# Thresholded attention with a gated mix: the phases of a product apart, and column tiles for attention's remainder

## The chip, the core and the metric

The kernel runs on one core of a Trainium2 chip, with TensorE (PE in the profile), VectorE (DVE), ScalarE (ACT), GpSimd (POOL) and SyncE (SP), which issues the DMAs. What counts is the device time of one execution in microseconds; the median of several runs is given.

## What is computed

Eight batches, eight heads of 576 positions with 64 values each. Attention keeps only the scores within `tau` of a row's largest; its output is the input of a gated mix with two 512x512 products.

```python
scores = scale * np.matmul(q, k.transpose(0, 1, 3, 2))
thresh = np.max(scores, axis=-1, keepdims=True) - tau
scores = np.where(scores >= thresh, scores, -1000000000.0)
attn = np.exp(scores - np.max(scores, axis=-1, keepdims=True))
attn = attn / (np.sum(attn, axis=-1, keepdims=True) + 1e-09)
x = np.matmul(attn, v)              # heads side by side: (B, S, 512)
for k in range(K):                  # K = 5, causal
    gate_pre += conv_w[k][None, None, :] * xp[:, k:k + S, :]
gate = 1.0 / (1.0 + np.exp(-gate_pre))
return gate * (x @ w_val) @ w_out
```

## The kernel before

A **job** is one pair of heads of one batch, 32 in all. Its rows of scores are worked on in tiles of 128 rows (288 tiles): PE makes a tile's scores out of `k` and `q` (line 572, two matmuls of 288 columns that run side by side, one on the upper 64 rows of the array and one on the lower, in two banks of one PSUM room), DVE scales them and finds the largest (579), ACT takes the exponential (593), DVE masks and sums (601), PE turns the result (686, transposes of 64 columns), ACT copies it to `T` (698, 702, 706), and PE multiplies `T` with `v`. That last product, **attention**, has four blocks of 128 keys for each of two heads, each with 64 columns of the array (lines 734 and 768), and a remainder of 64 keys a head, which stand together in one block of 128 and are multiplied by one matmul over all 128 columns (727 and 760). The first jobs do this half by half (`attended`), the jobs from tile 41 on with both halves at once (`attended_at_once`), in one PSUM room. DVE divides the result (740, 776), and ACT, DVE and POOL make its convolution (`convolve`), its gate, and two parts, `xh` and `xl`, whose sum is the value.

After the four jobs of a batch come eight **products** (`products`, line 923): four with `w_val` (`wv` in the program's names), then four with `w_out` (`wo`), each of 128 output features and both halves of the positions. A product is 48 matmuls of 64x128 weights and 288 columns, in pairs: one on the upper 64 rows of the array, one on the lower. As both write all 128 partitions, the two of a pair go to different banks, and every bank needs both. So there are two phases, `turn` 0 and 1: in the first the upper rows write bank 0 and the lower bank 1, in the second the other way round. Between the phases stands a drain of PE. Each phase is two operations of 6 pairs (`AT_ONCE = 2`), and each operation follows the one before (`last`), over products and batches, too. DVE then multiplies the product with the gate (959), or ACT or DVE scale it for the output (1023, 1025).

The order on every engine is set by a planner that runs while the program is built (`carry_out`). Each operation has an engine, a cost, operations that it follows, rooms that it takes and gives, and a due time: the number of its tile plus an offset from a table, `EARLY` for tiles under 69 and `AT` for the others. The planner lets its own clock run, and gives the engine that is free first the operation with the least due time of those that could begin. What it emits is fixed; on the chip every engine goes through its list in order and waits for semaphores. Four PSUM rooms of two banks, `u`, serve scores, transposes, attention and products alike. Several operations may go to one of two or three engines, as the small add that makes the threshold, `th`.

```python
cost = 0.39 * AT_ONCE + (DRAIN if turn and not c0 else 0.0)
last = [op("PE", k, cost, done, run, after, [] if turn or c0 else [r_acc])]
k += PACE_M
```

## Time and profile before

| | |
|---|---|
| median of 3 runs | 723.87 us (721.24 to 723.91) |
| the profiled execution | 722.67 us |
| its span, first to last instruction | 720.8 us |
| PE matmul busy | 683.0 us, 95% of the span |
| PE weight loads busy (PEld) | 524.4 us, 73% |
| DVE busy | 642.5 us, 89% |
| ACT busy | 514.3 us, 71% |
| POOL busy | 258.6 us, 36% |

Shares are of the whole span and mix stages with different limits: a start of about 140 us in which weights are prepared and the first jobs run, a long even stage, and an end of some 37 us with products alone. Matmuls are pipelined and their ends are modelled, so two that follow each other overlap in the records; what a piece costs PE is read from starts. The granted clock is 0.983 of full speed in the mean, 1.00 from 200 us on.

### The profile page before, as it was taken

How to read it: one execution, taken by the hardware profiler on the slowest of the kernel's cores; microseconds unless marked ns; L12 is line 12 of the kernel's file. 1: busy time of each engine (PE TensorE's matmuls, PEld its weight loads, DVE VectorE, ACT ScalarE, POOL GpSimd, SP SyncE). 2: the span in 40 equal slices, each digit the busy share in tenths (PEclk: the TensorE clock that was granted, in tenths of full speed). 3: DMA queues.
4: the chain of work that ended last, by engine and by line, in shares of the span. 5: the costliest groups of instructions: out<-in, count | busy, mean ns of one | idle time of the engine just before them, and what ended most of it. 6: DMA issues, size and time to landing. Idle time of an engine off the chain costs nothing.

```text
span 720.8 us, 21163 instructions
## 1 busy us (share of the span) xinstructions
PE 683.0 (95%) x8470; PEld 524.4 (73%) x8470; DVE 642.5 (89%) x1709; ACT 514.3 (71%) x937; POOL 258.6 (36%) x420
## 2 busy tenths in 40 slices
PE   8787789889999999999999999999999999999997
PEld 5444456667677787777777787777877877777887
DVE  6999789998899998899899998999999998999642
ACT  6887687777877787677776787777776877777520
POOL 2453444564223423324222432235123442234240
PEclk9998889999999999999999999999999999999999
DMA  7132313222222233221232233211332232220102
GB/s 257 49 111 94 111 56 100 69 83 99 68 83 83 68 113 116 82 83 50 86 115 71 77 106 109 100 47 56 109 104 83 84 99 88 70 77 3 51 17 67
DMA packets 21074, 61.17 MB, mean 85 GB/s; under 512 B 2928, under 2 KB 4336, under 8 KB 20976
## 3 DMA queue, kind: packets, MB, share of 16 engines
q1 hardware_dynamic: 20832, 59.62, 25.0%
q8 instruction: 67, 1.10, 0.6%
q14 instruction: 31, 0.25, 0.1%
q10 hardware_dynamic: 144, 0.20, 0.1%
HBM read 50.37 MB, written 9.44 MB: 83 GB/s over the span
## 4 chain that ended last, share of the span: by engine, by line
PE 73%; DVE 17%; issue 4%; ACT 3%; DVEq 0%; ACTq 0%
PE u L923 28%; PE u L572 18%; PE u L768 12%; PE u L686 10%; DVE sb L579 6%; DVE pp L601 5%; PE u L760 3%; DVE pre L834 2%; PE u L734 1%; DVE pl L601 1%; ACT e L593 1%; DVE g L959 1%; ACT T L698 1%; PE u L727 0%; ACT tmp L847 0%
## 5 line engine op out<-in xcount | busy, mean ns | idle before, releaser
L593 ACT ACTIVATE e<-sb,nm 128x576 f32<-128x576 f32 x288 | 223.3, 778 | 96.6 <-DVE pp L601 38.8
L579 DVE TENSOR_SCALAR_CACHE_REDUCE sb<-u,sc 128x576 f32<-128x576 f32 x288 | 228.4, 808 | 34.5 <-PE u L572 27.1
L601 DVE SCALAR_TENSOR_TENSOR pp<-sb,th,e 128x577 f32<-128x577 f32 x256 | 222.1, 875 | 2.2 <-ACT e L593 1.7
L572 PE MATMUL u<-k,q 64*128 64x288 f32 x1240 | 200.1, 424 | 4.0 <-ACT T L698 1.3
L698 ACT COPY T<-u 128x768 f32<-128x768 f32 (+1 forms) x256 | 169.4, 688 | 17.2 <-PE u L686 14.9
L686 PEld LDWEIGHTS u<-ident,pp 64*128 64x128 f32 x2304 | 101.2, 141 | 45.9 <-DVE sb L579 14.3
L686 PE MATMUL u<-ident,pp 64*128 64x64 f32 x2304 | 112.8, 227 | 16.3 <-DVE sb L579 10.5
L572 PEld LDWEIGHTS u<-k,q 64*128 64x128 f32 x1240 | 105.8, 190 | 22.6 <-ACT T L698 5.5
L768 PE MATMUL u<-T,v 128*64 128x320 f32 (+1 forms) x864 | 110.7, 409 | 0.0
L629 POOL TENSOR_SCALAR inv<-r 128x128 f32<-128x128 f32 x101 | 35.3, 350 | 209.6 <-DVE r L619 161.9
L834 DVE SCALAR_TENSOR_TENSOR pre<-xT,cw,pre 128x576 f32<-128x576 f32 x121 | 102.1, 843 | 1.1 <-POOL pre L829 0.9
L923 PE MATMUL u<-gh,woh 64*128 64x288 f32 x512 | 91.9, 351 | 5.0 <-ACT T L698 0.9
L923 PE MATMUL u<-xh,wvh 64*128 64x288 f32 x512 | 91.5, 350 | 3.4
L768 PEld LDWEIGHTS u<-T,v 128*64 128x64 f32 x864 | 59.7, 137 | 47.7 <-issue 9.0
L923 PE MATMUL u<-xh,wvl 64*128 64x288 f32 x512 | 76.9, 292 | 0.0
L923 PE MATMUL u<-xl,wvh 64*128 64x288 f32 x512 | 76.9, 292 | 0.0
L923 PE MATMUL u<-gh,wol 64*128 64x288 f32 x512 | 76.8, 291 | 0.0
L923 PE MATMUL u<-gl,woh 64*128 64x288 f32 x512 | 76.7, 291 | 0.0
L990 POOL TENSOR_TENSOR gl<-g,gh 128x288 fp32r<-128x288 f32 x64 | 57.1, 903 | 35.1 <-ACT gh L982 35.1
L923 PEld LDWEIGHTS u<-xh,wvh 64*128 64x128 f32 x512 | 49.7, 187 | 17.4 <-issue 14.5
L923 PEld LDWEIGHTS u<-gh,woh 64*128 64x128 f32 x512 | 49.3, 185 | 17.1 <-issue 12.3
L816 POOL TENSOR_TENSOR xl<-xT,xh 128x320 fp32r<-128x320 f32 x64 | 55.7, 888 | 3.2 <-ACT xh L810 2.7
(87 smaller groups left out, 894.0 us busy)
## 6 DMA issues: line engine op xcount, KB each, us to landing
q<-qT SPq DMA_DIRECT2D x31, 608.0 KB, 3.9
k<-kT SPq DMA_DIRECT2D x31, 496.0 KB, 5.3
v<-vs SPq DMA_DIRECT2D x32, 320.0 KB, 2.9
outT<-o SPq DMA_DIRECT2D x28, 288.0 KB, 2.2
pre<-w_val SPq DMA_DIRECT2D x4, 512.0 KB, 6.9
pre<-w_out SPq DMA_DIRECT2D x4, 512.0 KB, 4.2
outT<-o SPq DMA_DIRECT2D x8, 144.0 KB, 1.8
pp<-first SPq DMA_DIRECT2D x2, 192.0 KB, 2.9
```

Of the source, the lines that this page charges most:

```text
L572: nc.tensor.matmul(row(self.s)[:, a, :], t.q[rows, x : x + P], t.k[rows, k0 : k0 + HS], start=i == 0, stop=h is not None or i == 1, skip_g ...
L579: nc.vector.tensor_scalar(self.sb[:, :S].rearrange("p (a f) -> p a f", a=2), row(self.room()), sc, None, op0=ALU.mult, op1=ALU.min, accum_ ...
L593: nc.scalar.activation(self.e[:, :S], self.sb[:, :S], AF.Exp, bias=self.nm, scale=-1.0)
L601: nc.vector.scalar_tensor_tensor(grp.p[:, i * S : (i + 1) * S + 1], self.sb, self.th, self.e, op0=ALU.is_le, op1=ALU.mult, accum_out=grp.s ...
L629: nc.gpsimd.tensor_scalar(out, x, 1.0, 0.0, op0=ALU.mult, op1=ALU.add)
L686: nc.tensor.transpose(tp[:, r, i * APART_BY : i * APART_BY + D], x[rows, :], ident[rows, rows])
L698: engine(T[:, c0 : c0 + n, self.off : self.off + P].rearrange("p c (r q) -> p r c q", r=2), tp)
L768: nc.tensor.matmul(a[hs, : W[half.j]], t.v[:, c0 : c0 + D], half.T[:, h * NKC + c, 0 : W[half.j]], start=False, stop=c == NKC - 1, skip_gr ...
L816: engine.tensor_sub(x["l"][:, c], pair.xT[:, PAD + c.start : PAD + c.stop], x["h"][:, c].bitcast(F32))
L834: engine.scalar_tensor_tensor(cv, pair.xT[:, i + a : i + z], cw[:, g, i : i + 1], cv, op0=ALU.mult, op1=ALU.add)
L923: nc.tensor.matmul(made["room"][:, to, 0:HS], wt[rows, c, e * P : (e + 1) * P], moving(c, i)[rows, parts[j]], start=turn == c == n == 0, s ...
L990: engine.tensor_sub(gs[e][1][:, c], g[x][:, c], gs[e][0][:, c].bitcast(F32))
```

## The change

- A phase of a product is one operation of 12 pairs (`AT_ONCE = 4`). `last` is now two chains, one for each phase: an operation follows the last one of its own phase, so that phase one of the next product may stand ahead of phase two of this one.
- The drain is gone. Instead ScalarE copies the first column of both banks of the product's room, 128x2 values, to a tile `seen` that nobody reads, once phase one is done; phase two follows that copy. The copy has its own due time, `swap`.
- Attention's remainder is a fifth block like the four others, with one matmul of 64 columns for each head, at the end instead of the start.
- Planner's costs of seven kinds of operations and nearly all due times of both tables have new values; `PACE_M` goes from 1.09431 for an operation to 2.22709 for one of twice the size. Arithmetic is as before but for the place of the remainder in the sum.

```diff
-PACE_M = 1.09431
+PACE_M = 2.22709
...
-DRAIN = 0.15
-AT_ONCE = 2
+AT_ONCE = 4
...
 AT = dict(
-    fetch_q=-569.48, score=730.99, largest=22.97, lowest=-2556.9, weigh=-4960.28, keep=626.9,
+    swap=2765.51, fetch_q=-921.28, score=724.65, largest=525.02, lowest=-2701.89,
+    weigh=-6846.69, keep=945.08, add=80.1, inv=-1094.54, divide=-767.55, turn=-5449.98,
...
-            cost, shape = 0.97 if both else 0.49, ROWS
+            cost, shape = 1.03 if both else 0.54, ROWS
...
-                op("ACT", due_of(k, "weigh"), 0.636, 0.83, self.weigh, [largest], [r_e]),
+                op("ACT", due_of(k, "weigh"), 0.68, 0.86, self.weigh, [largest], [r_e]),
...
             for a, half in zip(acc, halves):
-                nc.tensor.matmul(
-                    a[:, : W[half.j]], t.v[:, NKC * P :], half.T[:, 2 * NKC, 0 : W[half.j]],
-                    start=True, stop=False, skip_group_check=True,
-                )
-            for a, half in zip(acc, halves):
-                for c in range(NKC):
+                for c in range(NKC + 1):
                     for h, hs in enumerate(HEADS):
                         c0 = (2 * c + h) * D
                         nc.tensor.matmul(
-                            a[hs, : W[half.j]], t.v[:, c0 : c0 + D], half.T[:, h * NKC + c, 0 : W[half.j]],
-                            start=False, stop=c == NKC - 1, skip_group_check=True,
+                            a[hs, : W[half.j]], t.v[:, c0 : c0 + D],
+                            half.T[:, 2 * NKC if c == NKC else h * NKC + c, 0 : W[half.j]],
+                            start=c == 0, stop=c == NKC, skip_group_check=True,
                         )
...
+            def swap():
+                nc.scalar.copy(seen, made["room"][:, :, 0])
+
             for turn in range(2):
                 for c0 in range(0, NE, AT_ONCE):
                     def run(turn=turn, c0=c0):
                         if turn == c0 == 0:
                             made["room"] = r_acc.take()
-                        if turn and not c0:
-                            nc.tensor.drain()
...
-                    after = [*(weights[name, c] for c in range(c0, c0 + AT_ONCE)), *last]
+                    after = [*(weights[name, c] for c in range(c0, c0 + AT_ONCE)), *last[turn], *swapped]
...
-                    cost = 0.39 * AT_ONCE + (DRAIN if turn and not c0 else 0.0)
-                    done = cost + 0.25 * (turn == 1 and c0 + AT_ONCE == NE)
-                    last = [op("PE", k, cost, done, run, after, [] if turn or c0 else [r_acc])]
+                    cost = 0.09 + 0.393 * AT_ONCE
+                    done = cost + 0.25 * (c0 + AT_ONCE == NE)
+                    last[turn] = [op("PE", k, cost, done, run, after, [] if turn or c0 else [r_acc])]
+                    if turn == 0 and c0 + AT_ONCE == NE:
+                        swapped = [op("ACT", due_of(k, "swap", k0), 0.19, 0.37, swap, last[0])]
                     k += PACE_M
```

The built order shows where the pieces stand. PE before, in the middle of the program, from the end of one product's phase one over the drain (which these rows leave out) to the start of its phase two; `u` are PSUM rooms, `gh` and `gl` the two parts of the gated value, `woh` and `wol` those of the weights, `ident` goes with transposes, `k` and `q` with scores:

```order
L923 MATMUL u_94<-gh_153,woh 128x288 x2
L923 MATMUL u_94<-gl_157,woh 128x288 x2
L923 MATMUL u_94<-gh_153,wol 128x288 x2
L923 MATMUL u_94<-gh_154,woh 128x288 x2
L923 MATMUL u_94<-gl_158,woh 128x288 x2
L923 MATMUL u_94<-gh_154,wol 128x288 x2
L572 MATMUL u_92<-k_97,q_99 128x288 x2
L686 MATMUL u_95<-ident,pp_116 128x64 x8
L923 MATMUL u_94<-gh_151,woh 128x288 x2
L923 MATMUL u_94<-gl_155,woh 128x288 x2
```

PE in the changed kernel at such a place, from the end of phase one to the start of phase two of one product:

```order
L918 MATMUL u_96<-xh_137,wvh 128x288 x2
L918 MATMUL u_96<-xl_146,wvh 128x288 x2
L918 MATMUL u_96<-xh_137,wvl 128x288 x2
L573 MATMUL u_95<-k_97,q_99 128x288 x2
L573 MATMUL u_94<-k_97,q_99 128x288 x2
L573 MATMUL u_93<-k_97,q_99 128x288 x2
L918 MATMUL u_96<-xh_139,wvh 128x288 x2
L918 MATMUL u_96<-xl_143,wvh 128x288 x2
```

Before, other work stood between any two of the four operations of 6 pairs, and the drain stood ahead of the third; now it stands between the two phases of 12 pairs, here three score groups.

PE before at one job's attention, between transposes and scores (`T` holds the turned rows, `v` the values):

```order
L572 MATMUL u_94<-k_97,q_99 128x288 x2
L760 MATMUL u_93<-T_0_129,v_100 128x320
L760 MATMUL u_93<-T_0_131,v_100 128x256
L768 MATMUL u_93<-T_0_129,v_100 64x320 x8
L768 MATMUL u_93<-T_0_131,v_100 64x256 x8
L686 MATMUL u_92<-ident,pp_117 128x64 x8
```

and in the changed kernel:

```order
L687 MATMUL u_94<-ident,inv_128 128x64 x2
L687 MATMUL u_96<-ident,pp_117 128x64 x8
L760 MATMUL u_93<-T_1_131,v_102 64x320 x10
L760 MATMUL u_93<-T_1_133,v_102 64x256 x10
L687 MATMUL u_94<-ident,pp_117 128x64 x10
```

The two matmuls of 128 columns are gone, and the others of 64 columns are 20 instead of 16.

ScalarE before, around the cast of a product's first gated value (`e` exponentials, `th` thresholds, `gh` that cast):

```order
L593 ACTIVATE e1_103<-sb2_106,nm1_108 128x576
L587 ACTIVATE th1_112<-nm1_108,less_87 128x1
L593 ACTIVATE e0_102<-sb0_104,nm2_109 128x576
L698 COPY T256_1_132<-u2_94 128x2x4x64
L982 CAST gh0_151<-g0_149 128x576
```

and in the changed kernel, with the copy to `seen` of the product before that:

```order
L594 ACTIVATE e0_103<-sb0_105,nm0_108 128x576
L906 COPY seen_88<-u3_96 128x2
L594 ACTIVATE e1_104<-sb1_106,nm3_111 128x576
L588 ACTIVATE th1_113<-nm1_109,less_87 128x1
L594 ACTIVATE e0_103<-sb2_107,nm1_109 128x576
L699 COPY T320_1_131<-u2_95 128x2x6x64
L699 COPY T256_1_133<-u1_94 128x2x4x64
L979 CAST gh0_152<-g0_150 128x576
```

The copy to `seen` stands between two exponentials.

## Rows read from the trace of the kernel before

**Rows 1.** Busy time by stage: stretch, its length, engines with instruction counts, clock, DMA.

```profile
core 0: us, PE busy (x) PEld busy (x) DVE busy (x) ACT busy (x) POOL busy (x), PEclk, DMA share, GB/s
0.00:140.00 140.00, 115.89 (x1174) 76.48 (x1174) 125.64 (x362) 104.85 (x189) 61.45 (x85) 0.93 0.32 109
140.00:200.00 60.00, 56.66 (x688) 42.44 (x688) 53.65 (x144) 46.91 (x85) 26.92 (x35) 0.97 0.26 84
200.00:660.00 460.00, 454.46 (x5875) 357.57 (x5872) 432.68 (x1142) 344.23 (x633) 154.34 (x280) 1.00 0.26 84
...
684.00:721.00 37.00, 32.39 (x444) 29.51 (x440) 11.92 (x23) 4.66 (x10) 9.04 (x11) 1.00 0.12 42
```

**Rows 2.** Waits of DVE from 200 to 660 us: total, times, longest.

```profile
DVE sb L579 <- PE u L572: 20.2, 29, 1.8
DVE xT L776 <- PE u L768: 1.6, 6, 0.3
```

**Rows 3.** Waits of the weight loads: whole span, then 200 to 660 us.

```profile
PEld u L923 <- issue: 26.8, 66, 0.6
...
PEld u L923 <- issue: 20.1, 45, 0.6
```

**Rows 4.** Order of time on PE near the end: start, length, instructions.

```profile
714.77 0.30 PE L923 MATMUL u<-gl,woh 64*128 64x288 f32 x2
714.90 0.30 PE L923 MATMUL u<-gh,wol 64*128 64x288 f32 x2
715.28 0.40 PE L923 MATMUL u<-gh,woh 64*128 64x288 f32 x2
715.52 0.30 PE L923 MATMUL u<-gl,woh 64*128 64x288 f32 x2
```

**Rows 5.** The same in the middle, without (first two) and with the drain.

```profile
314.78 0.67 PE L572 MATMUL u<-k,q 64*128 64x288 f32 x4
...
315.39 0.32 PE L923 MATMUL u<-xl,wvh 64*128 64x288 f32 x2
...
316.05 0.68 PE L572 MATMUL u<-k,q 64*128 64x288 f32 x4
...
317.07 0.30 PE L923 MATMUL u<-xl,wvh 64*128 64x288 f32 x2
```

**Rows 6.** The chain that ended last, about 611 to 624 us: start, length.

```profile
611.43 0.48 PE u L572 x4
...
617.91 1.17 PE u L760 x4
619.07 4.03 PE u L768 x32
623.10 0.77 PE u L686 x20
```

**Rows 7.** Attention's column matmuls, 200 to 660 us: group by line.

```profile
L768 PE MATMUL u<-T,v 128*64 128x320 f32 (+1 forms) x704 | 90.2, 409 | 0.0
```

**Rows 8.** ScalarE's groups by line and shape, whole span: busy us, mean ns.

```profile
L593 ACT ACTIVATE e<-sb,nm 128x576 f32<-128x576 f32 x288 | 223.3, 778 | 96.6 <-DVE pp L601 38.8 <-DVE sb L579 36.6 <-DVE r L619 20.0
...
L706 ACT COPY T<-u 64x128 f32<-64x128 f32 x64 | 16.7, 261 | 0.4
...
L332 ACT ACTIVATE cw<-cw_raw 128x20 fp32r<-128x20 f32 x1 | 0.2, 204 | 0.0
```

**Rows 9.** An early half's attention on PE, in order of time.

```profile
93.72 0.93 PE L727 MATMUL u<-T,v 128*128 128x256 f32 x2
94.57 1.95 PE L734 MATMUL u<-T,v 128*64 128x256 f32 x16
96.45 0.76 PE L572 MATMUL u<-k,q 64*128 64x288 f32 x4
```

**Rows 10.** A transpose and the copy in ScalarE that waited for it.

```profile
304.88 0.23 PE L686 MATMUL u<-ident,inv 64*128 64x64 f32 x2
...
305.15 0.80 ACT L698 COPY T<-u 128x768 f32<-128x768 f32 x1 [0.18 <-PE u L686]
```

More of the change, by code (lines that the diff above doesn't have):

```diff
@@ L68 @@
+    products=740.47, val=-2564.64, g_high=2432.14, g_low=683.44, out=-294.52, send=-4968.7,
+    words=552.34, words_step=87.13, words_fetch=2543.61, split=-698.62, words_sub=-857.56,
+    words2=323.19, cw=-3470.99, corner=3365.88,
 )
@@ L655, in turned @@
                     half.room = [turn]
-                cost = 0.89 if self.both else 0.07 + 0.1 * m
+                cost = 1.0 if self.both else 0.07 + 0.1 * m
                 out.append(op(
@@ L759, in attend @@
             for a, half in zip(acc, halves):
[L760 to L765 removed]
+                for c in range(NKC + 1):
                     for h, hs in enumerate(HEADS):
```

51 lines of the change are left out of this document (22 added, 29 removed).

## The prediction

> **What bounds the kernel now.** I read the stages first, then who waits for whom, then TensorE (PE) instruction by instruction, since a matmul's end in the profile is modelled and its busy share hides holes.
>
> The stages [rows 1]: from 200 to 660 us PE is busy 454.46 of 460.00 us (99%), VectorE (DVE) 432.68 (94%), ScalarE (ACT) 344.23 (75%). Before 140 us DVE leads (125.64 of 140.00 against PE's 115.89). From 684 us on PE works nearly alone (32.39 of 37.00). The granted clock is 1.00 from 200 us on, the 2.4 GHz level, so nothing is to be had from the clock there.
>
> In the long stage DVE is idle for 460.00 - 432.68 = 27.3 us, and 20.2 + 1.6 = 21.8 of these end with a PE matmul [rows 2]: PE is the later engine, but DVE is only 6% behind it. That sets the scale: PE can be relieved of about as much as the change removes before DVE takes over.
>
> PE's 99% holds holes. PE's weight loads sat idle ahead of a product's matmul, for nothing that the profile shows, 66 times for 26.8 us in all, 45 of them in the long stage [rows 3]. The kernel has 8 batches x 8 products = 64 drains. They are the holes.
>
> **The change part by part.**
>
> *The drain.* Near the end [rows 4], product pairs start every 0.13 us (714.77, 714.90). Across the drain the next starts are 715.28 and 715.52: from 714.90 to the second pair 0.62 us instead of 2 x 0.13 = 0.26, so the drain costs 0.36 us. In the middle [rows 5]: from a score group's start to the second pair of the product behind it 315.39 - 314.78 = 0.61 us without the drain, 317.07 - 316.05 = 1.02 with it: 0.41 us. The weight loader says the same: 26.8 / 66 = 0.41. I take 0.36, the cleaner place. In the long stage 45 x 0.36 = 16.2 us of PE; over the run 64 x 0.36 = 23.0 (26.2 at 0.41).
>
> *Blocks of 12 pairs.* The matmuls are as many as before and pairs cost 0.13 us in a block of either length. Without a drain, score group to product costs 0.61 us, which is the scores' own 0.48 [rows 6] and one pair's step: a change of operation costs PE nothing there, so fewer, longer blocks save nothing either. Cost zero. What it moves: a score group that was due can now wait 12 x 0.13 = 1.6 us behind a block instead of 0.8.
>
> *Attention's remainder.* One product of a job with both halves: 619.07 - 617.91 = 1.16 us for the two full-width matmuls, then 623.10 - 619.07 = 4.03 for 8 column pairs of each width, 5.19 in all [rows 6]. After, there are 10 pairs for 8: at most 4.03 x 20/16 = 5.04. At 0.24 us a pass it is 4.03 + 4 x 0.24 = 4.99. Saved 0.15 to 0.20, say 0.18. The column matmuls of the long stage are 704 records [rows 7], 32 to a job, so 22 jobs: 22 x 0.18 = 4.0 us. The ten early halves save more each (0.85 + 1.88 = 2.73 us against 1.88 x 20/16 = 2.35, [rows 9]), up to 3.8 us together, but where DVE leads.
>
> *The copy in ScalarE.* 64 new instructions. None of its shape is in the trace: the nearest are 204 ns (128x20) and 261 ns (64x128, also out of PSUM) [rows 8]. I take 0.24, so 64 x 0.24 = 15 us. The built order also gives ACT fewer of the small threshold adds (98 to 62; VectorE 117 to 124, GpSimd 73 to 102), so its load hardly moves, and DVE's rises by 7 small operations, 1.5 us. ACT is 25% idle in the long stage; the time itself lies beside other work.
> By the Trainium skill, "ScalarE: Activation LUTs", section "What ACT_TABLE_LOAD costs", an ACTIVATE with immediate operands takes 186 ns + 0.833 ns an element, which would make the copy 188 ns and the sum 12 us. No run here shows that copy yet.
>
> *The wait that comes instead.* Phase two now waits for PE's last phase-one matmul, ACT and the copy. The matmul lasts 0.30 us [rows 4]. ACT picked up a transpose 0.04 us after its modelled end (304.88 + 0.23 against 305.15, [rows 10]). With the copy and as much again for the way back this is 0.30 + 0.04 + 0.24 + 0.04 = 0.62 us from the last start, if ACT is free. The cover is what stands between the phases: in the built order two score groups (2 x 0.48 = 0.96 us) at the least in the long stage, mostly three pieces (score groups, or transposes at 0.77 / 20 = 0.04 each, [rows 6]), 1.0 to 1.8 us, about 1.25 in the mean. Slack 0.34 at least, 0.6 in the mean. ACT takes its instructions in order, and an exponential holds it for 0.78 us [rows 8], so at 75% load some copies come late: I allow 0.1 us each, from 0 to 0.3. Behind the copy in ACT's queue stand the next exponentials, for which DVE's masking waits; behind the waiting phase in PE's queue everything. The end of the program has two exceptions: its very last product has nothing between its phases (0.62 - 0.13 against 0.36 now, so 0.1 to 0.2 us worse), the others there have another product's whole phase as cover.
>
> *The tables.* All due times are new, so every engine's order shifts. Bound from the stage where they decide most, before 200 us, where DVE is idle (140.00 - 125.64) + (60.00 - 53.65) = 20.7 us [rows 1]: a better order could win some of this back, a worse one lose as much. I take 0 and keep 5 us to each side, a quarter of that idle time.
>
> **The sum.** Long stage: PE's own work now is 454.46 less 16.2 + 4.0, which is 434.3 us; DVE's stays 432.7 + 1. Neither can reach its floor while each waits for the other: of DVE's 5.9% idle I give half, 3%, to both (13 us of PE, in which the late copies, 45 x 0.1 = 4.5, are included). 434.3 / 0.97 = 447.7, a gain of 12.3 us. End: 9 drains x 0.36 = 3.2, two jobs of attention 0.4, less 0.2 for the last product and 0.3 for late inputs: 3.1. Start: about 10 drains and the early halves, 3.6 + 3.8 of PE where DVE leads: a fifth, 1.5. Together 16.9 us, so the span goes from 720.8 to 703.9, and with the 722.67 - 720.80 = 1.87 us around it to 705.8 us. The median of the runs shown, 723.87, lies 1.2 above the profiled execution: **707 us**.
>
> **The rivals.**
>
> *DVE takes over at once.* The holes were slack that DVE did not need: it is busy 94% and its waits for PE are single ones (29 of them, up to 1.8 us, [rows 2]), which come from where a score stands in the queue, and 1.6 us blocks make such places worse. If DVE keeps 5% idle, the long stage is 432.7 / 0.95 = 455.5, a gain of 4.5; with 3.1 at the end the time is 716.3 us. For it: DVE's load is unchanged. Against it: PE has no idle time but its holes, and nearly all of DVE's idle time is a wait for PE.
> This is what the Trainium skill would expect ("Perfetto Trace Analysis", section "Identifying the Most-Contended Engine"): matmul busy time is no measure of TensorE, weight loading is, and the engine with the highest occupancy is to be relieved. By the rows that is 357.57 of 460 us (78%) against DVE's 94%, so DVE. The trace agrees on the first half, as the holes show; on the second, PE's queue is what DVE waits for. I give it 0.18.
>
> *The copy comes late: slower.* One mechanism: ACT stands in an exponential and the next, or a transposed copy, is ahead of the copy; the way is then 0.62 + 0.78 + 0.7 = 2.1 us against a cover of 1.25, so PE stands 0.85 us where the drain cost 0.36. Price (0.85 - 0.36) x 64 = 31 us, less 4 from attention: 750 us. It decides from a mean lateness of 0.36 + 4.0/45 = 0.45 us of PE per product on. For it: ACT is 75% busy and in order. Against: its idle time comes in pieces spread over the stage, and the copy stands where phase one ends. 0.07.
>
> *Nothing measurable.* The new order loses in the first 200 us (where DVE leads, so drains are worth little) 8 to 12 us, and the gain of 17 shrinks to 5 or 8 with a DVE half taken over: 720 to 727 us. The same number comes if the copy is late by just the drain's cost, the change then not removing what it says. 0.10.
>
> *Both floors reached.* All 20.2 us of PE in the long stage, 3.2 at the end and 4 at the start, better tables: 695 us. 0.05.
>
> **How the numbers follow.** The forecast (698 to 713) holds 0.60, the four others 0.18, 0.07, 0.10, 0.05. The range takes in the first rival and the bounds of the late copies (0.3 x 64 = 19 us of PE, about 12 on the path) and of the tables on the forecast: 697 to 719. Above it lie the slower rival and most of the neutral one (0.13), below it the floors (0.05). 0.5% of 723.87 is 3.6 us, about what a measurement of this kernel can tell from no change: faster than 720.25 has 0.60 + 0.05 + 0.18 = 0.83, slower than 727.5 0.07, the rest 0.10.
>
> **What would show it.** In the profile after: no idle of the weight loads for "issue" ahead of products (26.8 us now); PE's waits for the copy in ScalarE under 10 us in all; attention in one group at 5.0 us a job; DVE's share in the long stage up from 94% to 96 or 97%, its waits for score matmuls down from 20 us to some 10. Right but too large, if DVE stays at 95% with waits for scores of over 15 us. Wrong, if PE waits for the copy over 20 us, or if the stretch before 200 us grows by more than 5 us.

## The result and the profile after

The changed kernel takes 715.57 us (median of 4 runs, 712.44 to 717.10), the kernel before 722.95 beside it: ratio 0.9895, interval 0.9853 to 0.9937. That is 1.05% faster: the sign of the forecast, but less than half its size (2.3%, 707 us), and almost to the microsecond the time of the first rival, 716.3.

The profiled execution took 717.1 us, with a span of 715.3, which is 5.5 us under the 720.8 of the kernel before at like granted clock in the mean (0.982 and 0.983). Busy time by stage of the changed kernel (stretch, its length, engines with instruction counts, clock, DMA):

```profile
0.00:140.00 140.00, 120.21 (x1246) 79.43 (x1246) 129.87 (x369) 108.15 (x201) 68.69 (x89) 0.94 0.32 109
140.00:200.00 60.00, 56.39 (x728) 43.34 (x726) 56.14 (x147) 47.67 (x91) 26.60 (x39) 0.94 0.27 89
200.00:660.00 460.00, 446.32 (x5918) 356.11 (x5916) 435.05 (x1143) 344.78 (x646) 173.14 (x290) 1.00 0.25 83
```

Against [rows 1], PE's busy time in the long stage fell by 8.1 us (454.46 to 446.32), but DVE's rose only from 432.68 to 435.05: 94.6% busy, not 96 or 97. GpSimd (POOL) rose from 154.34 to 173.14. The granted clock is 1.00 there, the 2.4 GHz level, as before.

The page's chain of work that ended last, by engine and by line, changed hands:

```profile
DVE 46%; PE 33%; ACT 11%; issue 8%; DVEq 0%; ACTq 0%
DVE pp L602 17%; DVE sb L580 15%; PE u L918 11%; PE u L760 10%; DVE pre L827 6%; PE u L573 6%; ACT e L594 4%; PE u L687 4%; ACT T L699 3%; DVE g L956 2%; DVE pl L602 2%; PE u L731 2%; DVE r L620 1%; DVE th L590 1%; ACT xh L803 1%
```

Before, the page gave PE 73% and DVE 17%. The chain follows one path, so its shares are no measure of a limit; but they say where to look.

What DVE waits for from 200 to 660 us (total, times, longest):

```profile
DVE xT L769 <- PE u L760: 9.7, 11, 1.1
DVE sb L580 <- ACT T L699: 6.4, 11, 0.6
DVE pp L602 <- ACT seen L906: 3.5, 6, 0.6
DVE pp L602 <- ACT e L594: 1.1, 5, 0.2
```

The 20.2 us of waits for scores in [rows 2] are gone. In their place DVE waits 9.7 us for attention (1.6 in [rows 2]), once in two jobs, and for ScalarE. The weight loads' idle time ahead of products for nothing that the profile shows, 26.8 us in 66 places in [rows 3], is 0.4 us in one place: the drains' holes are gone.

The stage repeats itself batch by batch. Its pace is read from one row in each, the evacuation of a batch's fourth and last job (DVE's division out of PSUM, into `xT`), which recurs at the same place (changed kernel; start, length):

```profile
267.06 0.82 DVE L769 TENSOR_TENSOR xT<-u,T 128x320 f32<-128x320 f32 x2 [1.01 <-PE u L760]
350.09 0.82 DVE L769 TENSOR_TENSOR xT<-u,T 128x320 f32<-128x320 f32 x2 [1.02 <-PE u L760]
433.11 0.82 DVE L769 TENSOR_TENSOR xT<-u,T 128x320 f32<-128x320 f32 x2 [1.03 <-PE u L760]
```

and in the kernel before:

```profile
272.51 0.82 DVE L776 TENSOR_TENSOR xT<-u,T 128x320 f32<-128x320 f32 x2 [0.28 <-PE u L768]
355.22 0.82 DVE L776 TENSOR_TENSOR xT<-u,T 128x320 f32<-128x320 f32 x2 [0.27 <-PE u L768]
437.93 0.82 DVE L776 TENSOR_TENSOR xT<-u,T 128x320 f32<-128x320 f32 x2 [0.27 <-PE u L768]
```

A steady batch takes 350.09 - 267.06 = 83.0 us after, 355.22 - 272.51 = 82.7 before. **The stage in which 16 us of drains were to be had got 0.3 us a batch slower.** Cut at the evacuation that ends the second batch's jobs, the one that ends the seventh's, and the end of the span, the kernel before has 191.6 + 412.6 + 116.6 us and the changed one 185.8 + 414.2 + 115.3. So the difference of -5.5 us is -5.8 at the start, +1.6 in the stage and -1.3 in the last batch and the end. Below, "batch" is this steady length, the clearest number of this study: it agrees to 0.1 us from one batch to the next in most kernels, and the granted clock is 1.00 there. The first batches, and with them the totals, differ by some us from run to run, and most of that goes with the granted clock before 200 us (see `after_again`).

### The profile page after: what moved, and what is told of

It reads as the page before. It is cut to its first block, busy times and chain, and to the rows that moved or that the text cites. A ratio compares the mean times of both kernels' runs of the same rounds, so it can differ in the third digit from the quotient of the medians.

```text
span 715.3 us, 21419 instructions
## 1 busy us (share of the span) xinstructions
PE 673.1 (94%) x8606; PEld 524.5 (73%) x8606; DVE 649.1 (91%) x1717; ACT 519.3 (73%) x979; POOL 282.3 (39%) x434
## 4 chain that ended last, share of the span: by engine, by line
DVE 46%; PE 33%; ACT 11%; issue 8%; DVEq 0%; ACTq 0%
DVE pp L602 17%; DVE sb L580 15%; PE u L918 11%; PE u L760 10%; DVE pre L827 6%; PE u L573 6%; ACT e L594 4%; PE u L687 4%; ACT T L699 3%; DVE g L956 2%; DVE pl L602 2%; PE u L731 2%; DVE r L620 1%; DVE th L590 1%; ACT xh L803 1%
## 5 line engine op out<-in xcount | busy, mean ns | idle before, releaser
L602 DVE SCALAR_TENSOR_TENSOR pp<-sb,th,e 128x577 f32<-128x577 f32 x256 | 227.6, 895 | 6.9 <-ACT seen L906 4.1
L699 ACT COPY T<-u 128x768 f32<-128x768 f32 (+1 forms) x256 | 170.6, 689 | 16.9 <-PE u L687 15.8
L573 PEld LDWEIGHTS u<-k,q 64*128 64x128 f32 x1240 | 108.4, 191 | 43.0 <-ACT T L699 16.7
L760 PE MATMUL u<-T,v 128*64 128x256 f32 (+1 forms) x1080 | 138.0, 410 | 0.7 <-ACT T L699 0.3
L760 PEld LDWEIGHTS u<-T,v 128*64 128x64 f32 x1080 | 75.5, 138 | 55.8 <-ACT gh L979 2.3
L827 DVE SCALAR_TENSOR_TENSOR pre<-xT,cw,pre 128x576 f32<-128x576 f32 x121 | 105.4, 871 | 0.6
L918 PE MATMUL u<-xh,wvh 64*128 64x288 f32 x512 | 88.3, 333 | 1.9 <-ACT T L699 0.8
L918 PE MATMUL u<-gh,woh 64*128 64x288 f32 x512 | 85.3, 322 | 0.7 <-ACT seen L906 0.3
L590 POOL TENSOR_SCALAR th<-nm,less 128x1 f32<-128x1 f32 x102 | 30.2, 297 | 100.8 <-DVE sb L580 51.3
L809 POOL TENSOR_TENSOR xl<-xT,xh 128x320 fp32r<-128x320 f32 x64 | 67.5, 1069 | 0.0
L630 POOL TENSOR_SCALAR inv<-r 128x128 f32<-128x128 f32 x82 | 32.8, 400 | 54.9 <-DVE r L620 31.8
```

The source lines that it names most:

```text
L573: nc.tensor.matmul(row(self.s)[:, a, :], t.q[rows, x : x + P], t.k[rows, k0 : k0 + HS], start=i == 0, stop=h is not None or i == 1, skip_g ...
L590: engine.tensor_scalar(self.th, self.nm, 1.0, less, op0=ALU.mult, op1=ALU.add)
L602: nc.vector.scalar_tensor_tensor(grp.p[:, i * S : (i + 1) * S + 1], self.sb, self.th, self.e, op0=ALU.is_le, op1=ALU.mult, accum_out=grp.s ...
L699: engine(T[:, c0 : c0 + n, self.off : self.off + P].rearrange("p c (r q) -> p r c q", r=2), tp)
L760: nc.tensor.matmul(a[hs, : W[half.j]], t.v[:, c0 : c0 + D], half.T[:, 2 * NKC if c == NKC else h * NKC + c, 0 : W[half.j]], start=c == 0, ...
L809: engine.tensor_sub(x["l"][:, c], pair.xT[:, PAD + c.start : PAD + c.stop], x["h"][:, c].bitcast(F32))
```

## The experiments

The question was where the long stage's 12 us went. DVE might have taken over at once (the first rival); the copies or the long blocks might cost what the drains did; or the new order of all engines, which the prediction put at zero, might cost it.

**What a drain is worth in each order.** `after_drain` puts the drain back into the changed kernel, ahead of phase two. `before_nodrain` takes it from the kernel before, where the second phase then writes the banks of the first.

```diff
 after_drain
+                        if turn and not c0:
+                            nc.tensor.drain()
 before_nodrain
-                        if turn and not c0:
-                            nc.tensor.drain()
...
-                                    to = r ^ turn
+                                    to = r
```

> The changed kernel with the drain put back ahead of phase two, its copy in ScalarE and its order kept: PE has 0.36 us more to do per product, 8 products a batch. Theory (VectorE sets the pace of the changed kernel, PE has slack): a steady batch, 83.0 us now, grows by under 1.5 us, and the whole by under 10 us, most of it at the end where products run alone. Rival (PE still sets the pace): 8 x 0.36 = 2.9 us a batch, 64 x 0.36 = 23 us in all, 739 us.

> The kernel before without its 64 drains, order and due times kept. So that no drain is needed, phase two writes the same banks as phase one, which leaves the sums of both phases in the wrong halves of the output; instructions and sizes are the same. Theory (VectorE is so close behind PE that it takes over at once): the steady batch falls from 82.7 us by at most 1 us and the whole gains 3 us at the end and a little before, 716 to 720 us. Rival (the drains were PE time on the path, and the new order lost what they gave): 2.9 us a batch, the whole near 702 us.

Measured: 723.13 us (ratio 0.9995, 0.9977 to 1.0012) with the drain back, 723.13 - 715.57 = 7.6 us above the changed kernel's median; 712.27 us (0.9837, 0.9813 to 0.9860) without it in the kernel before, 12 us below the 724.22 beside it. The medians mix runs of different granted clock. At 0.995 in the mean the changed kernel takes 712.6 us (four runs, `after_again` included) and with the drain 722.2 (three): 9.6 us. At 0.986 to 0.988 the kernel before takes 721 to 724 us and without the drain 711.8 and 712.0: about 11. The batch went up by 0.9 us (83.0 to 83.9) and down by 0.9 (82.7 to 81.8), as the first theory of either run has it; the total of `before_nodrain` fell by more than it said. A batch has 8 drains, 8 x 0.36 = 2.9 us of PE. In either order a third of it reaches the batch's length.

**How much of it DVE holds.** `after_light` and `before_light` cut the last tap of the convolution on DVE from a whole row to 64 columns, which takes 0.28 us instead of 0.84: with four last taps to a batch some 2.2 us less of DVE.

```diff
+                w = a + 64 if i == KT - 1 else z
...
-                    cv, pair.xT[:, i + a : i + z], cw[:, g, i : i + 1], cv, op0=ALU.mult, op1=ALU.add
+                    cv, pair.xT[:, i + a : i + w], cw[:, g, i : i + 1], cv, op0=ALU.mult, op1=ALU.add
```

> The changed kernel with the last of the four convolution taps on VectorE cut from 576 columns to 64 (the rest of that tap is left out), order kept: VectorE has some 0.55 us less to do per job, 2.2 us a batch. Theory (VectorE sets the pace): the batch of 83.0 us falls by 1.5 to 2.2 us, the whole by 10 to 16 us, near 701 us. Rival (PE, or a chain over several engines, sets the pace): under 0.7 us a batch, 710 us or more.

> The kernel before with the same tap cut to 64 columns, order kept. Theory (PE with its drains set the pace of the kernel before): the batch of 82.7 us falls by under 0.7 us, the whole by under 6 us. Rival (VectorE set the pace there, too, and the drains never counted): 1.5 to 2.2 us a batch, near 709 us.

Measured: 707.16 us (0.9758, 0.9733 to 0.9784) and 720.86 (0.9956, 0.9933 to 0.9979). The batch fell by 1.0 us (83.0 to 82.0) after, and by 0.2 (82.7 to 82.5) before. The 1.0 lies between the theory (1.5 to 2.2) and its rival (under 0.7). DVE's load hardly counted before, and in the changed kernel half of it does, beside a third of PE's (`after_drain`): the bound moved towards DVE, but neither sets the pace alone.

**The copy and its wait.** `after_noswap` takes out the copies, with what makes them needed (phase two on the banks of phase one).

```diff
             def swap():
-                nc.scalar.copy(seen, made["room"][:, :, 0])
+                pass
...
-                                    to = r ^ turn
+                                    to = r
```

> The changed kernel without the copy in ScalarE and without the wait for it, order otherwise kept. So that phases need no order, phase two writes the same banks as phase one, which leaves the sums of both phases in the wrong halves of the output. Theory A (the copies are what was given back: they hold up exponentials in ScalarE's queue, and PE): the steady batch falls from 83.0 us to about 81.8, where the kernel before without drains stands, the whole by 8 to 10 us. Theory B (the new order of work, with blocks of 12 pairs and new due times, is what was given back): at most 0.4 us a batch, the whole by under 4 us.

Measured: 713.00 us (0.9862, 0.9845 to 0.9879), the batch unchanged at 83.0. The copies cost the stage nothing. The 2.6 us of the total lie in the first batches and go with the granted clock: at 0.995 in the mean the changed kernel takes 712.2 to 713.2 us (four runs) and `after_noswap` 712.9 to 713.1 (three). In the trace of the changed kernel PE waits 0.6 us in all for the copy, its weight loads 1.6. DVE's 3.5 us "for `seen`" are waits for the exponential next to it: without copies the row reads `DVE pp <- ACT e`, 4.9 us, against 3.5 + 1.1.

**The tables or the operations.** `after_oldtables` gives the changed kernel the due times of before (`swap` as in the changed kernel, `PACE_M` twice 1.09431), `before_newtables` the kernel before the new ones (`PACE_M` half of 2.22709).

> The changed kernel's code and costs with the due times of the kernel before (and the new ones for the copy, and half the step of the products twice as long). Theory B (the order gave it back): the steady batch comes out clearly different from 83.0 us, by over 1 us to either side. Theory A (the copies): within 0.5 us of 83.0.

> The kernel before, drains, 6-pair operations, full-width remainder and costs kept, with the due times of the changed kernel. If the new due times alone brought what was won at the start (97.0 to 93.4 and 94.7 to 92.4 us in the first two batches), these two batches show it here, too. Theory B: the steady batch moves from 82.7 us by over 1 us.

Measured: 724.93 us (1.0042, 1.0017 to 1.0067), batch 84.7; and 740.73 (1.0232, 1.0210 to 1.0254), batch 84.8. Due times and operations fit only as a pair: neither run tells what either is worth, but together they show that an order moves this kernel by 9 to 18 us, as much as the drains or more. My 5 us to each side for it was too narrow.

**Both reliefs in the old order.** `before_cols` has the column tiles alone; `before_nodrain_cols` has them and no drain, as above. No due time or cost differs from the kernel before.

```diff
-                for c in range(NKC):
+                for c in range(NKC + 1):
...
-                            half.T[:, h * NKC + c, 0 : W[half.j]],
+                            half.T[:, 2 * NKC if c == NKC else h * NKC + c, 0 : W[half.j]],
```

> The kernel before with attention's remainder in column tiles, nothing else. PE has 0.18 us less to do per job, 0.7 us a batch. If a third of PE's relief reaches the path, as it did for the drains (0.9 of 2.9 us a batch), the steady batch falls from 82.7 by 0.2 to 0.3 us, the first two batches by up to 1 us each, and the whole by 2 to 4 us. If attention's place is on the path in every job, 0.7 us a batch and 5 to 7 us in all.

> The kernel before with both reliefs of PE at once: no drains (phase two writes the same banks as phase one, the sums of both phases in the wrong halves of the output) and the remainder of attention in column tiles; its order and due times kept. Theory (both reliefs add up, and only the new order took back what the changed kernel lacks): steady batch 82.7 - 0.9 - 0.4 = 81.4 us, the whole by 10 + 5 us lower, near 707 us. Rival (VectorE's floor is reached by one of them): batch 81.8 or little less, 711 us.

Measured: 717.75 us (0.9925, 0.9903 to 0.9947), batch 82.3, and 707.61 us (0.9792, 0.9774 to 0.9810), batch 81.2. Here is the forecast's 707, without the new order (and, as phase two writes the banks of phase one, without any order between the phases). The batch of `before_cols` fell by 0.4 us, more than a third of PE's 0.7. Span 705.6 against 720.8, cut as above: 188.3 + 404.7 + 112.6, so -3.3, -7.9 and -4.0. The new order then takes back: 185.8 - 188.3 = -2.5 at the start, 414.2 - 404.7 = +9.5 in the stage, 115.3 - 112.6 = +2.7 at the end, +9.7 us in all.

DVE from 200 to 650 us in `before_nodrain_cols` (busy, mean ns, idle before and what ended it):

```profile
L579 DVE TENSOR_SCALAR_CACHE_REDUCE sb<-u,sc 128x576 f32<-128x576 f32 x199 | 158.3, 807 | 19.3 <-PE u L572 15.9 <-PE u L686 0.8 <-DVE pp L601 0.2
L601 DVE SCALAR_TENSOR_TENSOR pp<-sb,th,e 128x577 f32<-128x577 f32 x176 | 152.2, 871 | 0.2
L826 DVE SCALAR_TENSOR_TENSOR pre<-xT,cw,pre 128x576 f32<-128x576 f32 x90 | 76.1, 845 | 0.0
```

and in the changed kernel:

```profile
L580 DVE TENSOR_SCALAR_CACHE_REDUCE sb<-u,sc 128x576 f32<-128x576 f32 x195 | 154.7, 807 | 7.9 <-ACT T L699 6.4 <-DVE pp L602 0.8
L602 DVE SCALAR_TENSOR_TENSOR pp<-sb,th,e 128x577 f32<-128x577 f32 x173 | 151.5, 880 | 5.8 <-ACT seen L906 3.5 <-ACT e L594 1.1
L827 DVE SCALAR_TENSOR_TENSOR pre<-xT,cw,pre 128x576 f32<-128x576 f32 x87 | 76.3, 877 | 0.4
L769 DVE TENSOR_TENSOR xT<-u,T 128x320 f32<-128x320 f32 (+1 forms) x44 | 18.4, 448 | 9.7 <-PE u L760 9.7
```

The reading of scores takes 807 ns in both, but masking takes 880 ns instead of 871 and a tap 877 instead of 845: DVE does the same work more slowly. In the changed order it also waits at three kinds of places instead of one. Both kernels' engines over the same 450 us, `before_nodrain_cols` first:

```profile
200.00:650.00 450.00, 446.92 (x5930) 358.00 (x5928) 428.68 (x1134) 340.69 (x628) 153.55 (x278) 1.00 0.25 85
200.00:650.00 450.00, 436.66 (x5810) 349.56 (x5808) 425.20 (x1122) 337.95 (x632) 167.76 (x282) 1.00 0.26 85
```

DVE's busy share times the batch is 428.68 / 450 x 81.2 = 77.4 us of work in the old order, 425.20 / 450 x 83.0 = 78.4 in the new. Of the 1.8 us between the batches 1.0 is DVE's work by these shares, 0.8 its idle time; counted over four whole batches in the traces it is 1.2 and 0.6. The work: 32 maskings a batch at 9 ns more are 0.3, 16 taps at 32 ns more 0.5, and the thresholds that DVE has in these 450 us, 83 in 16.5 us instead of 72 in 14.8, another 0.3.

**Why DVE works more slowly.** GpSimd's differences, the subtractions that make the low parts `xl` and `gl`, are its longest work, and in the changed kernel they take longer, too (GpSimd, 200 to 650 us; first the changed kernel):

```profile
L809 POOL TENSOR_TENSOR xl<-xT,xh 128x320 fp32r<-128x320 f32 (+1 forms) x42 | 46.4, 1123 | 0.0
L987 POOL TENSOR_TENSOR gl<-g,gh 128x288 fp32r<-128x288 f32 x46 | 43.8, 971 | 21.2 <-ACT gh L979 21.2
```

The kernel before:

```profile
L990 POOL TENSOR_TENSOR gl<-g,gh 128x288 fp32r<-128x288 f32 x44 | 39.4, 904 | 23.1 <-ACT gh L982 23.1
L816 POOL TENSOR_TENSOR xl<-xT,xh 128x320 fp32r<-128x320 f32 (+1 forms) x42 | 36.5, 891 | 1.5 <-ACT xh L810 1.1
```

One place of the changed kernel shows how, in order of time (DVE and GpSimd, start and length):

```profile
249.04 0.81 DVE L602 SCALAR_TENSOR_TENSOR pp<-sb,th,e 128x577 f32<-128x577 f32 x1
249.23 1.23 POOL L822 TENSOR_SCALAR pre<-xT,cw 128x576 f32<-128x576 f32 x1 [4.47 <-DVE xT L769]
249.78 0.08 DVE L602 DVE_READ_ACCUMULATOR pp<-sb,th,e 128x1 f32 x1
249.78 1.29 DVE L602 SCALAR_TENSOR_TENSOR pp<-sb,th,e 128x577 f32<-128x577 f32 x1
250.43 1.22 POOL L809 TENSOR_TENSOR xl<-xT,xh 128x256 fp32r<-128x256 f32 x1
251.00 0.08 DVE L602 DVE_READ_ACCUMULATOR pp<-sb,th,e 128x1 f32 x1
251.00 0.15 DVE L620 RECIPROCAL r<-sums 128x2 f32<-128x2 f32 x1
251.08 0.79 DVE L580 TENSOR_SCALAR_CACHE_REDUCE sb<-u,sc 128x576 f32<-128x576 f32 x1
...
268.47 0.82 DVE L580 TENSOR_SCALAR_CACHE_REDUCE sb<-u,sc 128x576 f32<-128x576 f32 x1 [0.59 <-ACT T L699]
268.63 0.74 POOL L822 TENSOR_SCALAR pre<-xT,cw 128x576 f32<-128x576 f32 x1
```

GpSimd's first tap (L822) takes 0.74 us beside a reading of scores, which comes out of PSUM. Begun within a masking, which reads two tensors from SBUF, it takes 1.23, half a microsecond longer, about the rest of the masking that runs; the next masking, begun while GpSimd works, takes 1.29 instead of 0.81 and ends 0.6 us after GpSimd's tap; and the difference `xl` behind that takes longer again. They go one after the other, not side by side.
By the Trainium skill, "SBUF — State Buffer", section "Who interferes with whom", a VectorE instruction with two SBUF inputs contends with a GpSimd instruction that reads SBUF, and the port pair that the two engines share is an exclusive lock. The trace agrees, with the 0.5 us at either side.
The two hold each other up more often in the changed kernel: counted in its trace from 200 to 650 us, 49 of 280 maskings and taps take over 0.9 us, against 33 of 288 in `before_nodrain_cols`. Those with no GpSimd instruction beside them take 813 to 814 ns in the mean in both.

Three kernels take the differences away: both low parts, `xl` and `gl`, are left out and zeros are written instead, in the changed kernel (`after_zero_low`), the kernel before (`before_zero_low`), and `before_nodrain_cols` (`bnc_zero_low`).

```diff
-                engine.tensor_sub(
-                    x["l"][:, c], pair.xT[:, PAD + c.start : PAD + c.stop], x["h"][:, c].bitcast(F32)
-                )
+                nc.gpsimd.memset(x["l"][:, c].bitcast(F32), 0.0)
...
-                        engine.tensor_sub(gs[e][1][:, c], g[x][:, c], gs[e][0][:, c].bitcast(F32))
+                        nc.gpsimd.memset(gs[e][1][:, c].bitcast(F32), 0.0)
```

> The changed kernel with GpSimd's subtractions that make the low parts replaced by writing zeros (the low parts are left out of the products), order kept: GpSimd then hardly works beside VectorE's masking and convolution taps, which in the changed kernel take 963 and 1064 ns where GpSimd works beside them and 814 otherwise. Theory C (GpSimd beside VectorE is what the new order costs): the steady batch falls from 83.0 us by 1.2 us or more, to about 81.5. Theory D (the places of instructions in the queues, as the evacuation that waits for attention 9.7 us in the stage): by under 0.6 us.

> The kernel before with GpSimd's subtractions that make the low parts replaced by writing zeros (the low parts are left out of the products), order kept; the counterpart of the same cut in the changed kernel, where the batch fell from 83.0 to 80.7 us. Here GpSimd beside VectorE makes masking 862 and taps 840 ns in the mean instead of 814. Theory (VectorE sets the pace of the changed kernel, PE that of the one before): the batch of 82.7 us falls by under 0.8 us, the whole by under 6 us. Rival (VectorE slowed by GpSimd set the pace of both): 1.5 to 2.3 us a batch, 710 us or less.

> The order of the kernel before with column tiles and without the drain (its steady batch 81.2 us), and both low parts of the split left out: zeros are written where GpSimd subtracted (so xl and gl are not computed), and phase two writes the banks of phase one. The new order without the low parts has a batch of 80.7 us, the old one with drains 82.0. If what the new order loses is the slowing of DVE by GpSimd alone, both orders come out level once the differences are gone: a batch of about 80.7 us, span 702 to 704, total 704 to 706. If the new order also loses by where its operations stand (its waits for attention and for ScalarE), the old order keeps a lead without the differences, too: DVE's work falls by some 1.6 us a batch and the batch to 79.5 to 80.0, total 699 to 702. If GpSimd's slowing never reached the batch in the old order, it stays at 81.2, total about 707.

Measured, with the batch with and without the differences:

| | us | ratio | batch with | without |
|---|---|---|---|---|
| `after_zero_low` | 698.68 | 0.9673 (0.9657 to 0.9689) | 83.0 | 80.7 |
| `before_zero_low` | 717.88 | 0.9937 (0.9916 to 0.9958) | 82.7 | 82.0 |
| `bnc_zero_low` | 698.30 | 0.9676 (0.9635 to 0.9717) | 81.2 | 79.9 |

DVE in `after_zero_low`, 200 to 650 us:

```profile
L602 DVE SCALAR_TENSOR_TENSOR pp<-sb,th,e 128x577 f32<-128x577 f32 x180 | 149.2, 834 | 6.2 <-ACT e L594 5.0
L825 DVE SCALAR_TENSOR_TENSOR pre<-xT,cw,pre 128x576 f32<-128x576 f32 x88 | 71.5, 812 | 0.4
```

Masking fell from 880 to 834 ns and a tap from 877 to 812; in the kernel before (868 to 829, 840 to 812) and in `bnc_zero_low` (871 to 832, 845 to 814) to the same. In the six traces that this compares, no engine is seen to wait for GpSimd from 200 to 650 us, so the time saved is not a wait for the differences themselves. What it is worth depends on who sets the pace: 2.3 us a batch in the changed kernel, 0.7 in the kernel before, where PE with its drains is the later engine, 1.3 once the drains are out and the column tiles are in. Between the two orders without drains the lead of 83.0 - 81.2 = 1.8 us shrinks to 80.7 - 79.9 = 0.8. So, by this difference, 1.0 us a batch of the new order's loss is GpSimd holding up DVE (0.8 of it is seen in the maskings and taps above), and 0.8 is left without it. Over four whole batches 0.5 of that is DVE's busy time, the thresholds 0.2 of it, and 0.3 its idle time.

**The changed kernel once more.** `after_again` is the changed kernel as it is.

> The changed kernel once more, beside the others on one chip: 713 to 717 us. In its first profile the first batch of attention ended at 93.4 us, in two variants with the same order there at 89.3 and 89.4; if that is the run and not the variant, this one may show either.

Measured: 714.73 us (0.9882, 0.9855 to 0.9909), batch 83.0. The first two batches took 184.1 us instead of 185.8, the last and the end 116.5 instead of 115.3. What differs at the start is the granted clock: 0.94 in the mean before 140 us in the first profile, 0.99 in this one, 0.94 from 140 to 200 us and 1.00 behind that in both. The ten runs of the changed kernel sort the same way: 712.2 to 713.2 us at 0.995 over the whole span (four), 714.6 at 0.993, 716.2 to 717.7 at 0.982 to 0.992 (five). So a few us between totals say little where the clocks differ; the steady batch is free of it. The 1.2 us at the end are not explained here.

**Other orders.** `v1` has the copy, the two chains and the column tiles in the kernel before's order: 6 pairs to an operation, and its due times and costs. `v2` is `v1` with due times chosen anew, `v3` the changed kernel (12 pairs) with due times chosen anew, `v4` the kernel before with its drains, column tiles and due times chosen anew.

> The kernel before with the drain replaced by the copy in ScalarE, two chains of operations and column tiles for the remainder, but with operations of 6 pairs, the costs and the due times of before; the copy is due at once. In its order 0.6 to 1.6 us of other work stand between the phases in the steady stage, 1.1 in the mean. Theory (new due times and blocks of 12 pairs took the gain back): a steady batch of 81.2 to 82.0 us and 707 to 711 us in all. Rival (the copy, or work put between the phases, moves the order as much as new due times do): 83 us or more a batch, 718 us or more.

> Copy in ScalarE instead of the drain, two chains, 6-pair operations, column tiles, costs of before, and due times searched anew from those of before, so that the order repeats evenly from batch to batch and VectorE finds its next instruction ready. Theory (the places in the queues decide, the reliefs of PE are worth 15 us or more once the order suits them): a steady batch under 80.5 us, 700 us or less in all. Rival (VectorE's load is the floor at some 81 us, where the kernel before without drains and with column tiles stood): 81 us, 706 us or more.

> The changed kernel, 12-pair operations and all, with due times searched anew from its own in the same manner. If blocks of 12 pairs are what costs, it stays above 82 us a batch and 711 us; if its due times alone were unsuitable, it comes near v2.

> The kernel before with its drains, with column tiles, and due times searched anew from its own in the same manner: what the search gives by itself. If the order is the lever and drains matter little, near v2; if the drains bind once the order is even, 2 us a batch above v2 and 10 us or more in all, some 712 us.

Measured: `v1` 718.40 us (0.9936, 0.9919 to 0.9953), its batches uneven, 80.2 to 84.9 in the steady stage and 83.0 in the mean, as its rival had it; `v2` 714.24 (0.9881, 0.9862 to 0.9899), batch 82.0; `v3` 715.20 (0.9903, 0.9888 to 0.9917), batch 82.5; `v4` 719.15 (0.9944, 0.9924 to 0.9964), batch 82.6, no better than `before_cols`. Two chains let the planner move phases, and with old due times the rhythm is gone; `v5` below has copies too and keeps it, so the copies are not why. Blocks of 12 (`v3`) and of 6 (`v2`) come within 1 us of each other in total and 0.5 us a batch. With the old due times the difference is larger, 84.7 (`after_oldtables`) to 83.0 (`v1`), but there costs differ, too. So the price of long blocks, which the prediction put at zero, stays open. `v4` is 4.9 us above `v2`, between its two expectations. `v2` missed my theory of it (under 80.5 us a batch) in an instructive way. Its stretch from 200 to 650 us, and two lines of DVE there:

```profile
200.00:650.00 450.00, 438.32 (x5880) 352.11 (x5879) 432.03 (x1102) 358.62 (x753) 139.01 (x213) 1.00 0.25 85
```

```profile
L812 DVE SCALAR_TENSOR_TENSOR pre<-xT,cw,pre 128x576 f32<-128x576 f32 x88 | 79.4, 902 | 0.0
L587 DVE SCALAR_TENSOR_TENSOR pl<-sb,th,e 128x577 f32<-128x577 f32 x23 | 21.7, 942 | 0.0
```

DVE is busy 96%, the share that my prediction hoped for, but 432.03 / 450 x 82.0 = 78.7 us a batch: taps of 902 ns stretch its work. The busy share of an engine that another can block is not all work done.

**The old order with real copies.** `v5` keeps the order of every engine from the kernel before, with the column tiles, and puts ScalarE's copy behind phase one wherever PE's next operation is not the product's own second phase. That is so for 51 of the 64 products; the other 13 keep the drain.

```diff
+            def swap(following):
+                if following is not made["second"]:
+                    nc.scalar.copy(seen, made["room"][:, :, 0])
+                    made["seen"] = True
...
-                        if turn and not c0:
+                        if turn and not c0 and "seen" not in made:
```

> The order of the kernel before on every engine, with column tiles, and the copy in ScalarE instead of the drain wherever other work stands between the phases (51 of 64 products; the others keep the drain). Between the phases stand 0.25 to 1.33 us against a way of 0.5 to 0.6 us over ScalarE, so PE still stands up to 0.35 us in three of eight products of a batch. Without any drain this order gave 81.2 us a batch and 707.6 us. Theory (the reliefs hold where the order stays): 81.3 to 82.0 us a batch, 708 to 713 us, under the changed kernel. Rival (copies squeezed into ScalarE's queue cost as much as drains): 82.3 us or more, 716 us or more.

Measured: 712.53 us (0.9863, 0.9842 to 0.9884), faster than the kernel before and the fastest that leaves nothing out; against the changed kernel, 3.0 us lower by the medians, the intervals overlap. Two rows of its pace:

```profile
271.32 0.82 DVE L772 TENSOR_TENSOR xT<-u,T 128x320 f32<-128x320 f32 x2
352.56 0.82 DVE L772 TENSOR_TENSOR xT<-u,T 128x320 f32<-128x320 f32 x2
```

The batch is 352.56 - 271.32 = 81.2 us, that of `before_nodrain_cols`, and masking and taps are back at 869 and 841 ns. DVE, ACT and GpSimd go through the same instructions in the same order as in the kernel before, but for the copies. So in the stage a copy with other work as its cover is as cheap as no ordering at all, and 1.8 us of the changed kernel's batch come from its order, the blocks of 12 pairs included. The total stays 4.9 us above `before_nodrain_cols`: the first two batches took 192.4 us instead of 188.3 and the end 34.8 instead of 32.7. No copy stands before 137.6 us and none behind 669.2, so the drains that are left are there; but the granted clock before 140 us was 0.91 in this profile and 0.94 in the other, so how much of the start is the drains' is not shown.

## Why the prediction was wrong

**What bounds the kernel.** Right as far as it went: PE was the later engine, with the drains as its holes. In the kernel before DVE's relief was worth 0.2 us a batch (`before_light`), PE's 0.9 (`before_nodrain`). The scale, "about as much as the change removes before DVE takes over", was too generous: a third of the drains' time reached the batch, and 1.5 of 3.6 us with both reliefs, not the three fifths that the sum took (12.3 of 20.2 us). PE's busy share could not show this. Without drains PE does 2.9 us less work a batch and the batch is 0.9 us shorter, so about 2 us of waiting a batch came back, and yet PE is busy 447.39 of 450 us in `before_nodrain`. The likely reason, which no row shows directly, is that waits of a few tenths lie under the modelled ends.

**The drain, 0.36 us.** The duration is not contradicted, and the idle time of [rows 3] is gone but for 0.4 us. What a drain adds to the total, at like clock, is 9.6 / 64 = 0.15 us in the changed kernel and 11 / 64 = 0.17 in the kernel before.

**Attention.** Right. A whole job's attention in the changed kernel's chain, where 5.19 had been and 4.99 was forecast:

```profile
262.01 5.00 PE u L760 x40
281.94 5.07 PE u L760 x40
```

On its own it brought 722.76 - 717.75 = 5.0 us (`before_cols`), and 0.4 us a batch where PE saved 0.7.

**The copy and its wait.** Right, and cheaper. In the long stage:

```profile
L906 ACT COPY seen<-u 128x2 f32<-128x2 f32 x44 | 6.4, 145 | 0.0
```

145 ns, not the 240 that I took from the nearest rows; late copies cost PE 0.6 us, not 4.5.
By the Trainium skill, "ScalarE: Activation LUTs", section "What ACT_TABLE_LOAD costs", an ACTIVATE of that size would take 188 ns; the copy, in the trace a COPY out of PSUM, took 145, so the rule was closer than my rows, but too high.
The bare way, at the last product, where nothing covers it:

```profile
709.13 0.29 PE L918 MATMUL u<-gh,wol 64*128 64x288 f32 x2
709.74 0.40 PE L918 MATMUL u<-gh,woh 64*128 64x288 f32 x2 [0.31 <-ACT seen L906]
709.98 0.30 PE L918 MATMUL u<-gl,woh 64*128 64x288 f32 x2
```

0.61 us from start to start, where I had 0.62: 0.48 above a pair's step of 0.13. The drain's 0.36 in [rows 4] was taken to the second pair behind it, though. On one footing the copy's way is 0.85 us to the second pair (709.13 to 709.98) against the drain's 0.62: 0.23 us dearer at a bare place, not the 0.1 to 0.2 that I had from mixing the two.

**The tables: the step that failed.** "I take 0 and keep 5 us to each side." The new order cost 9.7 us against the same reliefs in the old order. That order is made by the due times together with the two chains, the planner's costs and the blocks of 12 pairs, which had a zero of their own in the sum ("Cost zero"); the runs show what it costs as a whole, and do not divide it among these. I had bounded it by the idle time before 200 us; but it gained there (2.5 us) and lost where an even stage repeats, 9.5 us over its five batches. I had counted which engine gets how many small adds, and did not ask what GpSimd's long instructions would then stand beside: they are as many as before (42 and 46 in the rows above, 42 and 44 before), but hold up DVE's maskings and taps more often. Of the 1.8 us a batch, 1.0 is DVE held up by GpSimd and 0.8 remains without that (`bnc_zero_low` against `after_zero_low`). DVE's largest wait in the new order is the one for attention:

```profile
346.37 3.67 PE L760 MATMUL u<-T,v 128*64 128x320 f32 x30
...
347.40 1.67 DVE L827 SCALAR_TENSOR_TENSOR pre<-xT,cw,pre 128x576 f32<-128x576 f32 x2
...
350.09 0.49 DVE L769 TENSOR_TENSOR xT<-u,T 128x320 f32<-128x320 f32 x1 [1.02 <-PE u L760]
```

DVE's list has the evacuation next, and PE still works at the product that it takes. Which of the moved operations lead to that, and how far this wait and those for ScalarE make up the 0.8 us, stays open: no run moves one due time alone.

**The sum.** Without its zero term it held: 16.9 us forecast, 15.2 measured in the old order (`before_nodrain_cols`), though spread otherwise: 1.5 forecast and 3.3 come at the start, where the granted clock was higher too (1.00 instead of 0.97 from 140 to 200 us); 12.3 for 460 us of the stage and 7.9 for the 412.6 between the cuts, which makes 8 to 9 for 460; 3.1 for the last 37 us and 4.0 for the last batch and the end. The agreement of the total is therefore in part luck.

**The rivals.** The first, DVE taking over at once, gave the right time by luck, and half of its reason: DVE's relief did become worth something. But DVE's load is not why the gain is missing, since the same reliefs bring the batch to 81.2 us in another order, where DVE has the same instructions but for a few adds. The late copy didn't come, though its price at a bare place was right. The neutral case named the cause, an order that loses 8 to 12 us, but put it before 200 us. Of the signs that I gave, the holes, PE's wait and attention came as said; DVE's share did not, and the waits for scores fell below my 10 us without any gain, since they had turned into other waits.

## What to carry to other kernels

An edit that comes with a new order of all engines is two edits: build the relief alone in the old order, and the order alone, before crediting either. A hole on a 99% engine is worth only what the engines close behind leave, here a third; ask with a small relief on each engine which of them a batch follows. When a planner moves work to an "idle" engine, look at whom that engine blocks.

## What the runs showed of the hardware

- GpSimd and DVE held each other up: masking of 0.81 us took 1.29, GpSimd's tap of 0.74 took 1.23, where each reads SBUF and DVE reads two tensors there. The reading of scores out of PSUM took 806 ns in the mean beside GpSimd and 809 without it, 820 at the most (changed kernel, 200 to 650 us). Without GpSimd's differences a batch of the changed kernel was 2.3 us shorter.
- Copying 128x2 values from PSUM in ScalarE takes 145 ns in the mean, and ordering PE against itself that way 0.61 us from start to start when nothing covers it, 0.23 us dearer than the drain; covered by other work, a batch with it was as long as one with no ordering (81.2 us in `v5` and `before_nodrain_cols`).
- The total of one kernel moved with the granted clock before 200 us: the changed kernel took 717.1 us at 0.982 in the mean over the span and 712.2 to 713.2 at 0.995.
